# Convolution blocks of 120 tokens with 8 rows of history, and the order of the first slot and of the last products

## The chip, the core and the metric

The kernel runs on one core of a Trainium2 chip. The metric is device time in microseconds (us) of the whole launch, by the median of its runs. A core has TensorE (PE in the rows; PEld is its weight load, which overlaps matmuls), VectorE (DVE), ScalarE (ACT), GpSimd (POOL) and SyncE (SP), which mainly starts transfers. The engines run at the same time, each through its own list of instructions, strictly in the order of that list; they wait for each other and for transfers by semaphores. SPq, ACTq and POOLq are the moments at which a transfer is issued.

## What is computed

A causal convolution over 7 tokens, with softmaxed taps for each of 8 heads, and behind it a routed feed-forward layer with 8 experts of which each token takes the best one:

```python
# x (8, 3584, 192), weight (8 heads, 7 taps)
w = softmax(weight)
out = np.einsum('hk,bskhg->bshg', w, x_unf)      # x_unf: windows of 7 tokens, zeros before the first
x = out.reshape(28672, 192)
logits = x @ w_gate + modality_bias[modality_id]
e_idx = np.argmax(logits, axis=1)
gate_w = softmax(logits)[np.arange(N), e_idx]
for e in range(8):
    h = np.maximum(x[e_idx == e] @ w1[e], 0.0)              # 192 -> 1024
    out[e_idx == e] = gate_w[e_idx == e, None] * (h @ w2[e])  # 1024 -> 192
```

All data is float32. With these inputs nearly all tokens go to experts 6 and 7 (14239 and 13901 of 28672; 532 go to expert 1).

## The kernel before, in words

**Tiles and groups.** A tile is a block of MB = 112 consecutive tokens of one of the 8 sequences, so 3584 / 112 = 32 blocks and 256 tiles. A load takes 4 tiles with 128 rows each: the block and the HALO = 16 rows ahead of it (`load_behind`, L273). The convolution is a matmul with a banded 128 x 112 matrix for each head. Tiles are worked in groups (class `Group`); QUADS_OF_GROUP (L22) gives the loads of each: 19 groups, the last 14 of them of 4 loads, 16 tiles. The first ten groups (WHOLE_X) multiply in plain float32 (`convolve_pair`, L318); the nine behind them split x into a high and a low part `xh`, `xl` and take three products for each head (`convolve`, L309). Then come the gate's logits (`turn`, `gate`, `logits`), the choice of expert (`choose`), a running count by which each token gets a row in a scratch tensor sorted by expert (`place`, two matmuls with `tri` and `ones`), and one indirect transfer for each tile that writes its rows there (`send`, L215, on POOL). The outputs y of the convolution lie in four buffers, each free again when its scatters have landed.

**Slots.** The feed-forward part runs in slots: one expert with 2, 4 or 1 passes of 256 rows, 114 passes in all. A slot loads its weights (`raw`, L674 to L679), splits each into a high and a low part (`w1b`, `w2b`; ACT casts, DVE subtracts, L103 and L104, eight parts, of which 0 to 3 are w1 and 4 to 7 are w2), and fetches its rows by lots of LOT = 2 passes (`bring`, L684: nine transfers, four `near`, four `far`, one `tags`). `turn` transposes a pass on DVE (`tp`) and splits it (`sxh`, `sxl`, `sxs`). A pass has 4 steps; each step has `first` (20 matmuls into `hps`, then `hh` on ACT and `hl` on DVE, of which the next but one step's `hps` needs the end, since there are two such banks) and, two steps later (LAG), `second` (16 matmuls into `po`). After a pass `put` scales its two tiles of 128 rows (`lowp` on ACT, `o` on DVE) and scatters them to the output (L791, on POOL).

**What sets the order.** The groups of chunk 0 (GROUPS_OF_CHUNK, four groups) are worked before the first slot; the others are dealt out over the steps of the slots that run meanwhile (`due`). On all engines a list scheduler sets the final order, except that ACT's is as written while slots run. SP issues weights, lots and x loads in one list: each lot stands behind the weights of the slot before which it was written. The kernel starts with `warm(WARM)`, 50 matmuls on constants, and has 20 more (WARM2) ahead of the first slot. `start(0)` splits parts 0 to 3 of the first slot, then deals out 26 pieces of group work, then turns pass 0; parts 4 to 7 follow behind the first `first`:

```python
for part in range(4 if i == 0 else 8):      # start
    made[i].split(part)
...
cur.first(p, fp)                            # run
if i == step == 0:
    for part in range(4, 8):
        cur.split(part)
...
for sl, *at in lagging:                     # the last two steps' second products
    sl.second(*at)
```

Of the kernel before, what the change touches and what calls it, by code (L numbers as in the profile page):

```python
# [9 lines left out]
F32 = mybir.dt.float32  # L10
F32R = mybir.dt.float32r
BF16 = mybir.dt.bfloat16
I32 = mybir.dt.int32
# [5 lines left out]
P = 128  # L19
MB = 112  # L20
HALO = 16
QUADS_OF_GROUP = (1, 1, 2, 2, 2) + (4,) * 14  # L22
WHOLE_X = 10
# [5 lines left out]
ORDERED = {mybir.EngineType.Activation}  # L29
WARM = 50  # L30
WARM2 = 20
# [4 lines left out]
T = 256  # L36
GROUPS_OF_CHUNK = (4, 3, 2, 2, 2, 2, 2, 2, 0, 0)
SLOTS_OF_CHUNK = (4, 3, 3, 4, 3, 4, 3, 3, 3)
# [8 lines left out]
def conv_then_routed_ffn(ctx, tc, x, weight, modality, w_gate, mod_bias, w1, w2, out):  # L47
    nc = tc.nc
    NB, S, D = x.shape
# [3 lines left out]
    N = NB * S  # L53
    NSB = S // MB
    NG = len(QUADS_OF_GROUP)
# [129 lines left out]
    def make_modality():  # L185
        both = const.tile([MB, 2, E], F32, name="both")
        nc.scalar.dma_start(out=both.rearrange("p m e -> p (m e)"),
                            in_=mod_bias.rearrange("m e -> (m e)").partition_broadcast(MB))
        step = const.tile([MB, E], F32, name="step")
        nc.vector.tensor_tensor(out=step, in0=both[:, 1, :], in1=both[:, 0, :], op=ALU.subtract)  # L190
        rows = N // MB
        ids = raw2[1].rearrange("p c d -> p (c d)")[:, 0:2 * MB * rows // P].bitcast(I32).rearrange("p (q s) -> p q s", s=2 * MB)
        nc.scalar.dma_start(out=ids, in_=modality.bitcast(I32).rearrange("(q p s) -> p q s", p=P, s=2 * MB))
        low = raw2[1].rearrange("p c d -> p (c d)")[:, 2 * MB * rows // P:3 * MB * rows // P].rearrange("p (q s) -> p q s", s=MB)
        nc.vector.tensor_copy(out=low, in_=ids.rearrange("p q (s two) -> p q s two", two=2)[:, :, ::-1, 0])
        mt_ps = ring(ps_t, 4, [MB, rows], F32, "mt_ps", "t")
        for q in range(rows // P):
            nc.tensor.transpose(out=mt_ps[:, q * P:(q + 1) * P], in_=low[:, q, :], identity=ident)
        mt = const.tile([MB, NB, NSB], F32, name="mt")
        with tc.issue_after(state["wg"]):  # L200
            nc.vector.tensor_copy(out=mt.rearrange("p b s -> p (b s)"), in_=mt_ps)
        return both[:, 0, :], step, mt
# [38 lines left out]
    class Group:  # L241


        def __init__(self, g, chunk):
# [13 lines left out]
            assert self.blocks * self.nb == self.tiles and self.b0 + self.nb <= NB  # L258

        def bank(self, use, *args):  # L260
# [12 lines left out]
        def load_behind(self, q, after_band):  # L273
            sb, b0 = self.block + q // 2, self.b0 + q % 2 * 4
            xr = self.x[:, 4 * q:4 * q + 4, :] if self.whole_x else ring(xp, 3, [P, 4, D], F32, "xr")
            if sb == 0:
# [102 lines left out]
        def choose(self):  # L379
# [22 lines left out]
            for i, y in enumerate(self.ys):  # L402
                nc.vector.reciprocal(out=y[0:MB, self.b0:self.b0 + self.nb, 0], in_=den[:, i * self.nb:(i + 1) * self.nb])
                with tc.issue_after(state["scatter"]) if "scatter" in state else nullcontext():
                    nc.gpsimd.iota(y.bitcast(I32)[0:MB, self.b0:self.b0 + self.nb, 1], pattern=[[S, self.nb]],
                                   base=self.b0 * S + (self.block + i) * MB + MB - 1,
                                   channel_multiplier=-1)

        def place(self):
# [4 lines left out]
            ohf = oh.rearrange("p t e -> p (t e)")  # L414
            nc.tensor.matmul(rp[:, 0].rearrange("p t e -> p (t e)"), tri, ohf, start=True, stop=True)
            nc.tensor.matmul(rp[:, 1].rearrange("p t e -> p (t e)"), ones, ohf, start=True, stop=True)
            ad = rt.tile([MB, E * NT], F32, name="ad", tag="ex", bufs=1)[:, 0:E * n].rearrange("p (e t) -> p e t", e=E)
# [20 lines left out]
        def send(self, t0, t1):  # L438
            for t in range(t0, t1):
                scatter(self.chunk, self.idx[:, t:t + 1], self.ys[t // NB][0:MB, self.b0 + t % NB, :])  # L440

# [220 lines left out]
    class Slot:  # L662


        def __init__(self, i, chunk, ent):
            self.i, self.h, self.passes, self.rows, self.ends, self.tags = i, {}, plan[chunk][2] // T, {}, {}, {}
            self.chunk, self.ent, load = chunk, ent, nc.sync
            with tc.issue_after(state["load"]) if "load" in state else nullcontext():
# [55 lines left out]
        def turn(self, k):  # L724
            lot, k0 = divmod(k, LOT)
            tp = ring(sp, 2, [P, NJ + 1, P], F32, "tp")
# [33 lines left out]

        def second(self, k, fp):
            wb = w2b[self.i % 2]
            hh, hl = self.h.pop((k, fp))
            if fp == 0:
                self.po = [ring(ps_g2, 2, [P, 2 * D], F32, "po") for _ in range(NJ)]
            for u in range(2):
                c = 2 * fp + u
                for j, po in enumerate(self.po):
                    js = slice(j * P, (j + 1) * P)
# [11 lines left out]
            if fp == NF // 2 - 1:  # L781
                self.put(self.h.pop(("tag", k)))

        def put(self, tag):
            for j, po in enumerate(self.po):
                gate = tag[:, j, 0:1]
# [10 lines left out]

    plan, tokens, slots, g = [], 0, 0, 0
    for chunk, groups in enumerate(GROUPS_OF_CHUNK):
        tokens += sum(QUADS_OF_GROUP[g:g + groups]) * 4 * MB  # L800
        g += groups
        size = PASSES_OF_SLOT[chunk] * T
        if chunk == len(GROUPS_OF_CHUNK) - 1:
# [69 lines left out]

    lots = [(i, lot) for i, (c, _) in enumerate(order) for lot in range(max(1, plan[c][2] // T // LOT))]

# [13 lines left out]
    def run(i0, i1):  # L889

        lagging, count = [], 0
        for i in range(i0, i1):
# [3 lines left out]
            for step in range(steps):  # L896
                p, fp = divmod(step, NF // 2)
                cur.first(p, fp)
                if i == step == 0:
                    for part in range(4, 8):  # L900
                        cur.split(part)
                lagging.append((cur, p, fp))
# [12 lines left out]
                if step >= (1 if late else 0) and order[far][0] in tables:  # L915
                    make(far)
                lot, end = lots.index((i, p // LOT)), sum(k < i1 for k, _ in lots) - 1
                if min(steps, NF) - step % NF <= 6 or sent(min(lot + 1, end)):
# [69 lines left out]
```

## Time and profile before

| | us |
|---|---|
| median of 3 runs (1249.28 to 1249.97) | 1249.29 |
| the profiled execution, its own time | 1249.29 |
| its span, first to last event | 1247.5 |
| PE busy in it | 1220.0 |
| DVE busy | 988.0 |
| ACT busy | 731.0 |
| POOL busy | 536.4 |

The rows further below come from this one execution. The busy time of PE is modelled: matmuls overlap, so the distance from one start to the next, or the share of the chain of waits, tells what a matmul costs the engine, not its own duration. [...] In the view of stretches the engine columns are busy us and, in brackets, instructions.

### The profile page before, as it was taken

Reading aid. Unit: us, or ns where it says so; the run is one execution under the profiler, and the core shown is the slowest. Engines: PE = TensorE matmul, PEld = TensorE weight load, DVE = VectorE, ACT = ScalarE, POOL = GpSimd, SP = SyncE. Lnnn points to the kernel's source line nnn. Section 1 sums busy time; section 2 is a strip of 40 time slices with the busy share of each in tenths; the row PEclk is TensorE's granted clock in tenths of the full one; section 3 lists DMA queues with packets and bytes.
Section 4 is the critical chain, followed back from the end, with each engine's and each line's share of the span. In section 5 each row is a group of like instructions: output and inputs, shape, how many; then the busy total and the mean of one; then the engine's idle time right before and its main releaser. Section 6 shows DMA issues by size and latency. Waiting matters only on the chain.

```text
span 1247.5 us, 28175 instructions
## 1 busy us (share of the span) xinstructions
PE 1220.0 (98%) x9254; PEld 1202.5 (96%) x9254; DVE 988.0 (79%) x2515; ACT 731.0 (59%) x1602; POOL 536.4 (43%) x564
## 2 busy tenths in 40 slices
PE   9899999999999999999999999999999999999996
PEld 7789999999999999999999999999999999999996
DVE  7688987878888778888888788877886676687894
ACT  2265665656666656665656556656655555556784
POOL 6647753535453453444545343452636221211221
PEclk9899999999999999999999999999999999999998
DMA  7687462543455335535552345423325334795541
GB/s 223 184 199 227 115 148 48 131 110 74 101 151 136 68 92 114 127 77 129 122 129 68 89 95 135 114 65 57 79 57 178 59 74 105 166 207 151 126 99 48
DMA packets 314016, 145.87 MB, mean 117 GB/s; under 512 B 225666, under 2 KB 300027, under 8 KB 313860
## 3 DMA queue, kind: packets, MB, share of 16 engines
q1 hardware_dynamic: 289396, 99.42, 36.7%
q0 software_dynamic: 23232, 44.30, 11.1%
q8 instruction: 74, 1.21, 0.4%
q14 instruction: 82, 0.67, 0.2%
q10 hardware_dynamic: 1232, 0.26, 0.1%
HBM read 118.16 MB, written 51.82 MB: 136 GB/s over the span
## 4 chain that ended last, share of the span: by engine, by line
PE 80%; DVE 8%; DMA 4%; issue 3%; ACT 2%; SPq 1%; POOL 0%; DVEq 0%; ACTq 0%; POOLq 0%
PE hps L752 37%; PE po L772 23%; PE po L776 11%; PE gt L365 4%; PE cv L309 3%; DMA raw<-in_moe_w_dram 2%; PE cv L325 2%; DVE hl L756 1%; DVE w1b L104 1%; DMA xr<-in_x_dram 1%; PE hps L118 1%; DMA routed_rows<-y,idx 1%; SPq L704 1%; DVE xl L104 1%; DVE tp L728 1%
## 5 line engine op out<-in xcount | busy, mean ns | idle before, releaser
L772 PE MATMUL po<-w2b,hh 128*128 128x384 f32 x1824 | 553.4, 354 | 0.9 <-DVE o L790 0.9
L752 PE MATMUL hps<-sxh,w1b 128*128 128x256 f32 x1824 | 481.5, 287 | 4.7 <-DVE hl L756 2.3
L756 DVE SCALAR_TENSOR_TENSOR hl<-hps,hh 128x512 fp32r<-128x512 f32 x456 | 311.2, 685 | 181.8 <-ACT hh L755 178.6
L755 ACT ACTIVATE hh<-hps 128x512 fp32r<-128x512 f32 x456 | 273.0, 599 | 310.3 <-PE hps L752 302.5
L776 PE MATMUL po<-w2b,hl 128*128 128x192 f32 x1824 | 441.7, 252 | 0.0
L215 POOL DMA_INDIRECT routed_rows<-y,idx x256 | 268.3, 1048 | 321.8 <-DVE hl L756 162.0
L791 POOL DMA_INDIRECT out_dram<-o,tags x228 | 239.1, 1049 | 370.2 <-DVE o L790 300.6
L752 PE MATMUL hps<-sxs,w1b 128*128 128x256 f32 x1824 | 363.0, 280 | 0.5 <-DVE sxs L739 0.5
L752 PEld LDWEIGHTS hps<-sxh,w1b 128*128 128x128 f32 x1824 | 343.9, 189 | 11.3 <-DVE hl L756 10.1
L776 PEld LDWEIGHTS po<-w2b,hl 128*128 128x128 f32 x1824 | 345.4, 190 | 0.0
L772 PEld LDWEIGHTS po<-w2b,hh 128*128 128x128 f32 x1824 | 343.9, 189 | 1.4 <-DVE o L790 1.1
L752 PEld LDWEIGHTS hps<-sxs,w1b 128*128 128x128 f32 x1824 | 279.8, 189 | 0.7 <-DVE sxs L739 0.7
L752 PE MATMUL hps<-sxl,w1b 128*128 128x256 f32 x912 | 255.8, 281 | 0.0
L752 PEld LDWEIGHTS hps<-sxl,w1b 128*128 128x128 f32 x912 | 172.8, 189 | 0.2 <-DVE sxl L739 0.2
L104 DVE TENSOR_TENSOR w1b<-raw,w1b 128x512 fp32r<-128x512 f32 x152 | 101.1, 675 | 11.1 <-ACT w1b L103 10.8
L788 ACT ACTIVATE lowp<-po,tags 128x192 f32<-128x192 f32 x228 | 83.6, 418 | 30.3 <-PE po L772 29.7
L103 ACT CAST w1b<-raw 128x512 fp32r<-128x512 f32 x152 | 92.4, 620 | 4.4 <-DMA raw<-in_moe_w_dram 3.7
L104 DVE TENSOR_TENSOR w2b<-raw,w2b 128x384 fp32r<-128x384 f32 x152 | 81.1, 543 | 12.0 <-ACT w2b L103 11.6
L790 DVE SCALAR_TENSOR_TENSOR o<-po,tags,lowp 128x192 f32<-128x192 f32 x228 | 84.3, 410 | 2.3 <-ACT lowp L788 2.3
L737 ACT CAST sxs<-tp 64x128 fp32r<-64x128 f32 x228 | 67.9, 298 | 30.1 <-DVE tp L730 27.3
L103 ACT CAST w2b<-raw 128x384 fp32r<-128x384 f32 x152 | 76.0, 512 | 1.0
L739 DVE TENSOR_TENSOR sxs<-tp,sxs 64x128 fp32r<-64x128 f32 x228 | 65.9, 289 | 9.0 <-ACT sxs L737 0.4
(138 smaller groups left out, 1020.8 us busy)
## 6 DMA issues: line engine op xcount, KB each, us to landing
raw<-in_moe_w_dram SPq DMA_DIRECT2D x38, 768.0 KB
raw<-in_moe_w_dram SPq DMA_DIRECT2D x38, 512.0 KB
raw<-in_moe_w_dram SPq DMA_DIRECT2D x76, 256.0 KB
xr<-in_x_dram SPq DMA_DIRECT2D x36, 384.0 KB
near<-routed_rows SPq DMA_DIRECT2D x212, 64.0 KB
x<-in_x_dram SPq DMA_DIRECT2D x26, 384.0 KB
routed_rows<-filler SPq DMA_DIRECT2D x9, 776.0 KB
far<-routed_rows SPq DMA_DIRECT2D x212, 32.0 KB
```

Of the source, the lines that this page charges most:

```text
L103: nc.scalar.copy(out=hi, in_=raw)
L104: return nc.vector.tensor_tensor(out=lo, in0=raw, in1=f(hi), op=ALU.subtract).ins
L215: state["scatter"] = nc.gpsimd.indirect_dma_start(out=scr, out_offset=bass.IndirectOffsetOnAxis(ap=idx, axis=0), in_=src, in_offset=None,).ins
L737: nc.scalar.copy(out=hi, in_=raw)
L752: nc.tensor.matmul(hps[:, u, :], wa[:, c, fs], mv[z], start=n == 0, stop=n == len(terms) - 1)
L755: nc.scalar.activation(out=hh, in_=hps, func=AF.Relu)
L756: hl_ins = nc.vector.scalar_tensor_tensor(out=hl, in0=hps, scalar=0.0, in1=f(hh), op0=ALU.max, op1=ALU.subtract)
L772: nc.tensor.matmul(po, hh[:, u, js], wb[:, c, :], start=c == 0, stop=c == NF - 1, skip_group_check=True)
L776: nc.tensor.matmul(po[:, 0:D], hl[:, u, js], wb[:, c, 0:D], start=False, stop=False, skip_group_check=True)
L788: nc.scalar.activation(out=lowp, in_=po[:, D:2 * D], func=AF.Copy, scale=gate)
L790: turn_behind(nc.vector.scalar_tensor_tensor(out=o, in0=po[:, 0:D], scalar=gate, in1=lowp, op0=ALU.mult, op1=ALU.add))
L791: st = nc.gpsimd.indirect_dma_start(out=out, out_offset=bass.IndirectOffsetOnAxis(ap=tag.bitcast(I32)[:, j, 1:2], axis=0), in_=o, in_offse ...
```

## The change

A block is now 120 tokens with 8 rows of history (the convolution needs 6). 3584 is no multiple of 120: there are 30 blocks, and the last one's rows end 16 short (CUT; 104 are left, ENDS). Its loads fill the missing rows with zeros by a memset on POOL, its counting matmuls take 104 rows, its scatters send 104. There are 240 tiles and 18 groups: one group of 16 tiles of the second kind (xh, xl) is gone, from the last chunk that has groups. The lookup of modalities is laid out anew (four transfers and a memset for one transfer). WARM is 42 for 50, and such a matmul now has 4 x 120 = 480 columns for 448. Slot 0 fetches its two passes as two lots of one pass each (`self.lot`), and all eight parts of its weights are split ahead of the group work in `start`. The two last steps' second products are worked by tile: all of tile 0, its `put`, then all of tile 1 and its `put`. The plan of slots keeps its size, 114 passes.

```diff
-MB = 112
-HALO = 16
-QUADS_OF_GROUP = (1, 1, 2, 2, 2) + (4,) * 14
+MB = 120
+HALO = 8
+QUADS_OF_GROUP = (1, 1, 2, 2, 2) + (4,) * 13
-WARM = 50
+WARM = 42
-GROUPS_OF_CHUNK = (4, 3, 2, 2, 2, 2, 2, 2, 0, 0)
+GROUPS_OF_CHUNK = (4, 3, 2, 2, 2, 2, 2, 1, 0, 0)
...
-    NSB = S // MB
+    NSB = -(-S // MB)
+    CUT = NSB * MB - S
+    ENDS = MB - CUT
...
+            if sb == NSB - 1:
+                nc.gpsimd.memset(xr[0:Q], 0.0)
+                ld = nc.sync.dma_start(out=xr[CUT:P], in_=x[b0:b0 + 4, sb * MB - HALO:S, :].rearrange("b s d -> s b d"))
...
+            for h, wt in enumerate((tri, ones)):
+                for lo, hi, rows in self.runs():
+                    nc.tensor.matmul(rp[:, h].rearrange("p t e -> p (t e)")[:, lo * E:hi * E], wt[0:rows], ohf[0:rows, lo * E:hi * E],
+                                     start=True, stop=True)
...
+            self.chunk, self.ent, self.lot, load = chunk, ent, 1 if i == 0 else LOT, nc.sync
...
-            k0, k1 = lot * LOT, min(lot * LOT + LOT, self.passes)
+            k0, k1 = lot * self.lot, min((lot + 1) * self.lot, self.passes)
...
-                if i == step == 0:
-                    for part in range(4, 8):
-                        cur.split(part)
...
-        for sl, *at in lagging:
-            sl.second(*at)
+        for j in range(NJ):
+            for sl, *at in lagging:
+                sl.second(*at, tiles=[j])
...
-        for part in range(4 if i == 0 else 8):
+        for part in range(8):
             made[i].split(part)
```

Three places show what this moves. Names: `w1b_89`, `w2b_91` and `raw_0` are the first slot's weights, `raw_1` the second's; line numbers are each kernel's own.

ACT, around the splits of the first slot, before:

```order
L328 COPY y_218<-cv 112x2x8x24 x3
L103 CAST w1b_89<-raw_0_85 128x512 x4
L328 COPY y_218<-cv 112x2x8x24
L737 CAST sxh<-tp 128x256
L737 CAST sxs<-tp 64x128 x2
L755 ACTIVATE hh<-hps 128x512
L103 CAST w2b_91<-raw_0_87 128x2x192 x4
L755 ACTIVATE hh<-hps 128x512
```

and in the change:

```order
L342 COPY y_202<-cv 120x2x8x24 x3
L105 CAST w1b_89<-raw_0_85 128x512 x4
L105 CAST w2b_91<-raw_0_87 128x2x192 x4
L342 COPY y_202<-cv 120x2x8x24
L759 CAST sxh<-tp 128x256
L759 CAST sxs<-tp 64x128 x2
L777 ACTIVATE hh<-hps 128x512 x2
L759 CAST sxh<-tp 128x256
```

The four casts of w2 moved from behind the first `hh` to a place ahead of a copy out of the convolution.

DVE, from the first slot's first `hl` on, before:

```order
L756 SCALAR_TENSOR_TENSOR hl<-hps,hh 128x512
L104 TENSOR_TENSOR w2b_91<-raw_0_87,w2b_91 128x2x192 x4
L756 SCALAR_TENSOR_TENSOR hl<-hps,hh 128x512
L728 STREAM_TRANSPOSE tp<-near 128x256
L730 STREAM_TRANSPOSE tp<-far 128x128
L739 TENSOR_TENSOR sxl<-tp,sxh 128x256
L739 TENSOR_TENSOR sxs<-tp,sxs 64x128 x2
L756 SCALAR_TENSOR_TENSOR hl<-hps,hh 128x512 x3
```

and in the change:

```order
L778 SCALAR_TENSOR_TENSOR hl<-hps,hh 128x512 x2
L750 STREAM_TRANSPOSE tp<-near 128x256
L761 TENSOR_TENSOR sxl<-tp,sxh 128x256
L752 STREAM_TRANSPOSE tp<-far 128x128
L761 TENSOR_TENSOR sxs<-tp,sxs 64x128 x2
L778 SCALAR_TENSOR_TENSOR hl<-hps,hh 128x512 x2
```

The subtractions for w2 are no longer between the first two `hl`; the turn of pass 1 (`tp` from `near` and `far`) still stands between the second `hl` and the third, but its rows are now those of a second lot.

SP, from the end of the first slot's first lot on, before (the lot of both passes ends with `tags`; what follows is slot 1):

```order
L704 DMA tags<-routed_rows 128x4x2
L669 TENSOR_LOAD tab
...
L674 DMA raw_1_86<-in_moe_w_dram 128x1024
...
L679 DMA raw_1_88<-in_moe_w_dram 128x8x192
L689 TENSOR_LOAD tab
...
L704 DMA near<-routed_rows 32x16x32
```

and in the change:

```order
L726 DMA tags<-routed_rows 128x2x2
L691 TENSOR_LOAD tab
...
L696 DMA raw_1_86<-in_moe_w_dram 128x1024
...
L701 DMA raw_1_88<-in_moe_w_dram 128x8x192
L711 TENSOR_LOAD tab
...
L726 DMA near<-routed_rows 32x8x32
```

The first `near` behind slot 1's weights now belongs to slot 0's pass 1 (32x8x32, half a lot), and slot 1's own lot (32x16x32) comes behind that.

## Rows read from the trace of the kernel before

**Rows 1.** The page: busy time of each engine, its share of the span, instructions.

```profile
PE 1220.0 (98%) x9254; PEld 1202.5 (96%) x9254; DVE 988.0 (79%) x2515; ACT 731.0 (59%) x1602; POOL 536.4 (43%) x564
```

**Rows 2.** Stretches of the span (from:to, length, then busy us of each engine with its instructions, granted clock, DMA share, GB/s).

```profile
48.00:53.30 5.30, 0.32 (x4) 0.12 (x2) 2.24 (x4) 2.65 (x5) 4.08 (x5) 0.91 1.03 312
...
140.00:1184.00 1044.00, 1041.20 (x7987) 1035.27 (x7986) 834.37 (x2040) 632.06 (x1382) 435.87 (x444) 1.00 0.46 108
```

**Rows 3.** The chain of waits in order of time, three pieces from the stretches 255 to 272 and 395 to 470: start, us on the chain, what (one counting matmul; the three products of one head; the twelve of one gate of 8 tiles).

```profile
271.35 0.06 PE rp L415
...
398.23 0.54 PE cv L309 x3
...
436.81 1.40 PE gt L365 x12
```

**Rows 4.** Groups of instructions by line and shape: the first of the three products of a head, nine groups by 8, and the gate's matmuls of the twelve later groups by 24.

```profile
L365 PE MATMUL gt<-gx,wg_parts 128*128 128x256 f32 x288 | 38.7, 282 | 1.8 <-DVE gx L104 1.5 <-ACT gx L103 0.3
...
L309 PE MATMUL cv<-xh,band_hi 128*112 128x384 f32 x72 | 25.4, 352 | 0.2 <-ACT xh L103 0.2
```

**Rows 5.** The end in order of time, on ACT, DVE and POOL: start, us, engine, line, operation, in brackets the idle time before it and its releaser.

```profile
1237.40 0.73 ACT L788 ACTIVATE lowp<-po,tags 128x192 f32<-128x192 f32 x2 [2.53 <-PE po L772]
1237.85 0.74 DVE L790 SCALAR_TENSOR_TENSOR o<-po,tags,lowp 128x192 f32<-128x192 f32 x2 [2.26 <-ACT lowp L788]
1238.55 0.98 POOL L791 DMA_INDIRECT out_dram<-o,tags  x1 [4.65 <-DVE o L790]
1239.83 0.99 POOL L791 DMA_INDIRECT out_dram<-o,tags  x1 [0.30 <-issue]
```

**Rows 6.** The start in order of time: the 50 warm-up matmuls, one weight load of them among the early ones, the 40 later ones, the loads of x behind the band matrices, the first convolutions.

```profile
1.16 11.88 PE L118 MATMUL hps<-ones 112*112 112x448 bf16 x50 [1.16 <-DVE ones L113]
...
3.82 0.22 PEld L118 LDWEIGHTS <-ones 112*112 112x112 bf16 x1 [0.16 <-issue]
...
4.19 0.22 PEld L118 LDWEIGHTS <-ones 112*112 112x112 bf16 x1 [0.16 <-issue]
...
4.57 8.06 PEld L118 LDWEIGHTS <-ones 112*112 112x112 bf16 x40 [0.16 <-issue]
...
11.12 3.25 SPq L280 DMA_DIRECT2D x<-in_x_dram  x6
...
13.10 3.29 PE L325 MATMUL cv<-x,band 128*112 128x96 f32 x32
```

**Rows 7.** POOL's scatters into the scratch rows in order of time: the first one, then the last two of chunk 0.

```profile
22.89 1.12 POOL L215 DMA_INDIRECT routed_rows<-y,idx  x1 [5.48 <-DVE ad L418]
...
51.92 0.94 POOL L215 DMA_INDIRECT routed_rows<-y,idx  x1 [0.30 <-issue]
53.17 1.29 POOL L215 DMA_INDIRECT routed_rows<-y,idx  x1 [0.30 <-issue]
```

**Rows 8.** SP's issues in order of time: slot 0's lot (near to tags), slot 1's weights, slot 1's lot.

```profile
56.18 2.04 SPq L704 DMA_DIRECT2D near<-routed_rows  x4
...
61.50 0.40 SPq L704 DMA_DIRECT2D tags<-routed_rows  x1
63.41 0.37 SPq L674 DMA_DIRECT2D raw<-in_moe_w_dram  x1
...
66.92 4.50 SPq L704 DMA_DIRECT2D near<-routed_rows  x4
...
74.16 0.39 SPq L704 DMA_DIRECT2D tags<-routed_rows  x1
```

**Rows 9.** ACT in order of time around the first slot.

```profile
51.70 1.14 ACT L103 CAST w1b<-raw 128x512 fp32r<-128x512 f32 x2 [2.34 <-DMA raw<-in_moe_w_dram]
52.74 0.47 ACT L328 COPY y<-cv 112x384 f32<-112x384 f32 x1
...
66.58 1.75 ACT L103 CAST w2b<-raw 128x384 fp32r<-128x384 f32 x4
```

**Rows 10.** DVE in order of time: pass 0's last transpose and subtractions, the first `hl`, pass 1's last transpose.

```profile
63.50 0.30 DVE L730 STREAM_TRANSPOSE tp<-far 128x128 f32<-128x128 f32 x1
64.17 0.61 DVE L739 TENSOR_TENSOR sxs<-tp,sxs 64x128 fp32r<-64x128 f32 x2 [0.36 <-ACT sxs L737]
66.59 0.69 DVE L756 SCALAR_TENSOR_TENSOR hl<-hps,hh 128x512 fp32r<-128x512 f32 x1 [1.81 <-ACT hh L755]
...
70.03 0.27 DVE L730 STREAM_TRANSPOSE tp<-far 128x128 f32<-128x128 f32 x1
```

**Rows 11.** PE in order of time: ten float32 convolution matmuls ahead of the first slot, the first matmul of step 2, the first of step 4 (pass 1).

```profile
60.54 1.79 PE L325 MATMUL cv<-x,band 128*112 128x192 f32 x10
...
67.34 0.39 PE L752 MATMUL hps<-sxh,w1b 128*128 128x256 f32 x1 [0.59 <-DVE hl L756]
...
72.47 0.39 PE L752 MATMUL hps<-sxh,w1b 128*128 128x256 f32 x1
```

**Rows 12.** Packets that the DMA engines moved from 64 to 71 us, then from 71 to 76.5 us (the rows of a lot are packets of 128 and 8 bytes, weights are packets of 4096 and 768 bytes).

```profile
DMA packets 1145, 1.69 MB, mean 242 GB/s; under 512 B 48, under 2 KB 889, under 8 KB 1145
...
DMA packets 4167, 0.97 MB, mean 177 GB/s; under 512 B 3824, under 2 KB 4087, under 8 KB 4167
```

**Rows 13.** PE alone, by stretches of 1 us: length, busy (instructions), granted clock, DMA share, GB/s.

```profile
58.00:59.00 1.00, 1.00 (x7) 0.50 1.03 208
59.00:60.00 1.00, 1.00 (x10) 0.90 0.76 112
```

More of the change, by code (lines that the diff above doesn't have):

```diff
@@ L258, in __init__, with rows @@
             assert self.blocks * self.nb == self.tiles and self.b0 + self.nb <= NB
+        def rows(self, i):
+            return ENDS if self.block + i == NSB - 1 else MB
         def bank(self, use, *args):
@@ L405, in choose, with runs @@
                     nc.gpsimd.iota(y.bitcast(I32)[0:MB, self.b0:self.b0 + self.nb, 1], pattern=[[S, self.nb]],
-                                   base=self.b0 * S + (self.block + i) * MB + MB - 1,
+                                   base=self.b0 * S + (self.block + i) * MB + self.rows(i) - 1,
                                    channel_multiplier=-1)
+        def runs(self):
+            if self.rows(self.blocks - 1) == MB:
+                return [(0, self.tiles, MB)]
+            return [(i * self.nb, (i + 1) * self.nb, self.rows(i)) for i in range(self.blocks)]
         def place(self):
@@ L439, in send @@
             for t in range(t0, t1):
-                scatter(self.chunk, self.idx[:, t:t + 1], self.ys[t // NB][0:MB, self.b0 + t % NB, :])
+                rows = self.rows(t // NB)
+                scatter(self.chunk, self.idx[0:rows, t:t + 1], self.ys[t // NB][0:rows, self.b0 + t % NB, :])
     chunk_of = [c for c, n in enumerate(GROUPS_OF_CHUNK) for _ in range(n)]
@@ L724, in turn @@
         def turn(self, k):
-            lot, k0 = divmod(k, LOT)
+            lot, k0 = divmod(k, self.lot)
             tp = ring(sp, 2, [P, NJ + 1, P], F32, "tp")
@@ L759, in first, with second @@
             self.h[k, fp] = hh, hl
-        def second(self, k, fp):
+        def second(self, k, fp, tiles=range(NJ)):
             wb = w2b[self.i % 2]
-            hh, hl = self.h.pop((k, fp))
-            if fp == 0:
+            hh, hl = self.h[k, fp]
+            if fp == 0 and tiles[0] == 0:
                 self.po = [ring(ps_g2, 2, [P, 2 * D], F32, "po") for _ in range(NJ)]
@@ L767, in second @@
                 c = 2 * fp + u
-                for j, po in enumerate(self.po):
+                for j, po in [(j, self.po[j]) for j in tiles]:
                     js = slice(j * P, (j + 1) * P)
@@ L781, in second, with put @@
             if fp == NF // 2 - 1:
-                self.put(self.h.pop(("tag", k)))
-        def put(self, tag):
-            for j, po in enumerate(self.po):
+                self.put(self.h["tag", k], tiles)
+        def put(self, tag, tiles):
+            for j, po in [(j, self.po[j]) for j in tiles]:
                 gate = tag[:, j, 0:1]
@@ L795, in put @@
                 tc.add_to_no_dep_group("out", st)
[L798 removed]
+    plan, tokens, slots, g, seen = [], 0, 0, 0, 0
     for chunk, groups in enumerate(GROUPS_OF_CHUNK):
[L800 removed]
         g += groups
+        brought = sum(QUADS_OF_GROUP[:g]) * 4 * MB - (CUT * NB if g == NG else 0)
+        tokens, seen = tokens + brought - seen, brought
         size = PASSES_OF_SLOT[chunk] * T
@@ L872, in make @@
             made.append(Slot(len(made), chunk, tables[chunk][:, k, :]))
-    lots = [(i, lot) for i, (c, _) in enumerate(order) for lot in range(max(1, plan[c][2] // T // LOT))]
+    lots = [(i, lot) for i, (c, _) in enumerate(order) for lot in range(max(1, plan[c][2] // T // (LOT if i else 1)))]
     def bring(n):
@@ L916, in run @@
                     make(far)
-                lot, end = lots.index((i, p // LOT)), sum(k < i1 for k, _ in lots) - 1
+                lot, end = lots.index((i, p // cur.lot)), sum(k < i1 for k, _ in lots) - 1
                 if min(steps, NF) - step % NF <= 6 or sent(min(lot + 1, end)):
```

27 lines of the change are left out of this document (15 added, 12 removed).

## The prediction

> **What bounds the kernel now.** I read the page's busy times first [rows 1]: PE is busy for 1220.0 of 1247.5 us, and the reader should see that no other engine comes near. Shares over the whole span hide stages, so the stretches come next [rows 2]: from 140 to 1184 PE is busy for 1041.2 of 1044.0 us while DVE has 834, so in the middle every matmul counts in full. What is left lies at the ends, and the sharpest piece is from 48.0 to 53.3, where PE does 0.32 us of work. The chain of waits [rows 3] gives the path's price of each piece of convolution work, and the groups by line and shape [rows 4] say how many there are. Then I read the two ends in order of time: the end on ACT, DVE and POOL [rows 5], the start on PE [rows 6], POOL's scatters [rows 7], SP's issues [rows 8], ACT, DVE and PE around the first slot [rows 9 to 11], and what the DMA engines move there [rows 12]. The clock row by row is last [rows 13].
>
> All terms are made against the profiled execution. Its own time, 1249.29, is also the median of the runs, and its span is 1247.5; I take the 1.8 us around the span as unchanged.
>
> **A group less.** The nine xh/xl groups make 72 high products, 8 each, and the twelve later groups 288 gate matmuls, 24 each [rows 4]. On the chain three products of a head cost 0.54 us, the twelve gate matmuls of 8 tiles 1.40, and a counting matmul 0.06 [rows 3]. One group is 8 × 0.54 + 2 × 1.40 + 2 × 0.06 = 7.24. It was worked while PE was full [rows 2], so it is on the path. The last group now takes four counting matmuls for two, +0.12. Columns per matmul don't change with the block (24 per tile), so the other groups cost what they did: **−7.1**. The passes stay 114. DVE, ACT and POOL lose the group's work too, under PE's cover. New there is a POOL memset ahead of each of two loads of the last groups, and SP, in order, waits with the weights and lots behind them. Loads run well ahead of their use, so I take 0; if that cover is gone I allow up to 2 us, from two scatter-sized POOL operations of about 1 us [rows 7].
>
> **The last products by tile.** Now both `o` are ready at about the same time, the second at 1237.85 + 0.74 = 1238.59, and POOL sends both behind that, at 1238.55 and 1239.83 [rows 5]. By tile, the first has gone by then, and the second can start as soon after its own `o` as POOL takes up a released scatter, about 0.3 us, at 1238.87. The matmuls are the same in number. 1239.83 − 1238.87: **−1.0**. Between 0 (the second `o` a microsecond later) and −1.3 (the distance of the two scatters).
>
> **The warm-up.** The early matmuls come 0.37 us apart (3.82 to 4.19), then 40 in 8.06 us, 0.20 each, and the convolutions start at 13.10 [rows 6]. With 480 columns for 448 these are 0.40 and 0.216; 42 of them end at about 11.8, 1.3 sooner. The x loads stand behind the band matrices and are issued at 11.12, and the first convolution follows warm-up without a wait, so I count the whole 1.3, though only for what hangs on it: POOL's chain of scatters. That chain runs from 22.89 to 54.46 with 24 scatters at a steady distance (1.25 us in the last two), and one of 112 rows takes 0.94 [rows 7] where one of 128 rows takes 0.98 to 0.99 [rows 5]. For 120 rows I add 0.02 each: +0.5. Slot 0's first `near`, issued at 56.18 [rows 8], comes at 56.18 − 1.3 + 0.5 = 55.4. The modality lookup is the last thing on PE ahead of the first convolution; with four transfers for one it may come later than the warm-up's end, and then this 1.3 is gone. Nothing waited there before, and I take 0.
>
> [...] No row of the kernel before shows a 120-row transfer.
>
> **The first slot's order.** Two things meet here.
>
> First, pass 0 comes sooner. Its lot is half as large. The full second lot, moved from about 71 to 76.5 as 4167 small packets [rows 12], tells that half of one saves up to 2.6 us; I take 2.0, since each transfer's own start is not halved. Pass 0's last transpose stood at 63.50 [rows 10]; 63.5 − 0.8 (the sooner issue) − 2.0 = 60.7. The four w2 casts (1.75 us [rows 9]) are now ahead of the copy of y that PE waits for at 53.3, and lengthen that idle time, but what ends last is still the rows of pass 0. Step 2's first matmul moves from 67.34 [rows 11] to about 64.8. The w2 splits no longer stand between the first two `hl`, which were at 66.59 and 69.07 at the far side of those subtractions.
>
> Second, pass 1 comes later. Its rows used to be in the one lot. Now they are behind slot 1's weights on SP. Those were issued at 63.41 [rows 8], and until 71 the DMA engines move hardly anything else: 1145 packets, 48 of them under 512 bytes [rows 12]. SP reaches them about 1.5 us sooner (0.8 and the shorter lot, whose issue gives less than its landing); they are through at 69.5, and half a lot behind them takes 2.6: 72.1. DVE and ACT stand in order at pass 1's transposes, so nothing of steps 2 and 3 behind them goes on either. From pass 1's last transpose at 70.03 [rows 10] to step 4's first matmul at 72.47 [rows 11] it took 2.44. So step 4 starts at 72.1 + 2.44 = 74.5, 2.0 later. By 64.8 + (72.47 − 67.34) = 69.9 PE is through with what stands ahead of it, and it waits some 4.5 us. At 74.5 PE has done less than at 72.47 before: of the ten float32 products ahead of the first slot, 1.79 us together [rows 11], six are not yet done (1.0), against two `po` products (0.35) done in advance, +0.6. Together **+2.6**; its ends are −1.9 (no wait, below) and +5.
>
> **Sum:** 1249.29 − 7.1 − 1.0 + 2.6 = **1243.8**.
>
> **Rivals.**
> *B, the wait also lowers the clock.* After the idle stretch up to 53.3 [rows 2] PE ran at 0.50 until about 59.15: the second from 58 to 59 has 0.50, the next 0.90 [rows 13]. So 5.9 us of matmuls ran at half speed, about 3.0 lost. A second idle stretch of 4.5 us behind step 3 is nearly as long as that one of 5.0. If it lowers the clock too: 1243.8 + 3.0 = 1246.8. Against it: the idle may come out shorter, or be broken by a few late products. [...]
>
> *C, pass 1 arrives in time.* Packets of the second lot may be let in between the weights' packets, or the weights be through sooner. For it: slot 1's lot was issued from 66.92 on [rows 8], well before the weights were through. Against it: of its packets hardly any came before 71 [rows 12]. Then step 4 starts at 69.9, 2.5 sooner than 72.47; with the 0.6: 1249.29 − 8.1 − 2.5 + 0.6 = 1239.3.
>
> *D, slower: the second lot lands much later.* Slot 1's weights go out as one block ahead of it, and x loads and scatters share the engines. If the rows of pass 1 land 5.0 us later than I say (77.1), and the clock drops as well, it is 1246.8 + 5.0 = 1251.8; without the drop it takes 8.0 us (80.1). Slot 1's whole lot, behind the same weights, was in by 76.5 [rows 12], so this is unlikely.
>
> *E, the change doesn't do what it says:* the group's 7.1 us come back as waits, because DVE (834 of 1044) or the loads set the pace where the group stood: 1249.29 − 1.0 + 2.6 = 1250.9.
>
> **How the numbers follow.** About 0.2%, 2.5 us, is what a measurement of this kernel can tell from no change: faster is under 1246.8, slower over 1251.8. A has 0.42, B 0.26 (it lies on the bound: half faster, half same), C 0.20, D 0.06, E 0.04, and 0.02 is for others, half faster and half same. Faster 0.42 + 0.13 + 0.20 + 0.01 = 0.76; same 0.13 + 0.04 + 0.01 = 0.18; slower 0.06. The range goes from just below C, 1238.8, to 0.8 above B, 1247.6, and leaves out D, E and what memset and landing times add to B.
>
> **What would show it.** Right: 64 high products where 72 stood, 264 gate matmuls; the first convolution at about 11.8; slot 0's first `near` at about 55.4; DVE idle ahead of pass 1's `tp`, released by its rows, and step 4's first matmul near 74.5; the last scatter 0.3 us behind its `o`. A granted clock of 0.50 between 74 and 80 is B. Step 4 by 71 is C. Wrong: PE idle over 3 us between 140 and 1184, or a step 4 beyond 77.

## The result, and the profile after

The changed kernel took 1258.54 us (median of 4 runs, 1258.1 to 1259.77), the kernel before 1249.63 on the same chip: a ratio of 1.0073, 95% interval 1.0061 to 1.0085. It is 8.9 us slower, where 5.5 us faster was forecast. The profiled execution took 1259.77, its span is 1258.1.

The page, PE's share, as [rows 1]:

```profile
PE 1218.9 (97%) x9198; PEld 1201.9 (96%) x9198; DVE 972.8 (77%) x2476; ACT 722.2 (57%) x1581; POOL 529.2 (42%) x546
```

The span grew by 10.6 us, and PE is idle for 11.7 more. Its busy time fell by only 1.1, although a group is gone, because more of it fell into stretches with a granted clock (PEclk, TensorE's, as a share of full speed) of 0.50: 19.0 us up to PE's last matmul, where the kernel before has 5.9, so some 6.5 us more were lost to the clock. The loss is at both ends. First the start on PE, as [rows 6], and then the instruction on DVE that PE waits for (start, us, engine, line, operation, in brackets idle time and its releaser):

```profile
1.17 11.55 PE L120 MATMUL hps<-ones 120*120 120x480 bf16 x42 [1.17 <-DVE ones L115]
18.77 0.62 PE L206 MATMUL mt_ps<-ident,raw 120*120 120x120 f32 x2 [6.05 <-DVE raw L203]
19.19 5.61 PE L339 MATMUL cv<-x,band 128*120 128x96 f32 x32
```

```profile
18.34 0.29 DVE L203 CAST raw<-raw 120x240 f32<-120x240 int32 x1 [9.97 <-DMA raw<-in_moe_modality_id_dram]
```

The convolutions start at 19.19, not 11.8: the modality ids are late. In the kernel before, their cast comes at 7.46, and the band matrices are issued at 7.56:

```profile
7.46 0.72 DVE L195 CAST raw<-raw 128x224 f32<-128x224 int32 x1 [0.35 <-DMA raw<-in_moe_modality_id_dram]
7.56 0.40 SPq L161 DMA_DIRECT2D band<-tap_lines  x1
```

The band matrices are now late as well. They are issued at 10.65, and the x loads behind their landing at 18.41 (11.12 before, [rows 6]), from SP in order of time:

```profile
10.65 0.40 SPq L163 DMA_DIRECT2D band<-tap_lines  x1
18.41 3.48 SPq L294 DMA_DIRECT2D x<-in_x_dram  x6
```

From 8 to 10 us the DMA engines move this and no more (packets, bytes, rate; then ACT's queue alone):

```profile
DMA packets 46, 0.05 MB, mean 26 GB/s; under 512 B 0, under 2 KB 45, under 8 KB 46
...
q10 hardware_dynamic: 45, 0.04, 6.2%
```

That is 45 packets of 960 bytes in 2 us, one every 44 ns: 6.2% of sixteen engines, about what one engine's share would be, a sixteenth or 6.25%. The view doesn't name the engine; that it is one is worked out from this share. From 14 to 18 us the last 65 packets of the band matrices (q1; 958 had gone from 11.8 to 14) and 64 packets of the ids (q10) take 6.9% together, again about one engine's share:

```profile
DMA packets 129, 0.09 MB, mean 23 GB/s; under 512 B 67, under 2 KB 129, under 8 KB 129
q10 hardware_dynamic: 64, 0.06, 4.3%
q1 hardware_dynamic: 65, 0.03, 2.6%
```

Behind these waits the granted clock of PE is lower. Stretches of PE (length, busy, granted clock, DMA share, GB/s):

```profile
16.00:18.00 2.00, 0.00 (x0) 0.70 0.07 22
...
20.00:22.00 2.00, 2.00 (x12) 0.50 0.96 318
...
58.00:59.00 1.00, 1.00 (x6) 0.50 0.92 228
...
65.00:66.00 1.00, 0.54 (x2) 0.50 0.35 93
...
84.00:85.00 1.00, 0.00 (x0) 1.00 0.15 2
86.00:87.00 1.00, 0.34 (x1) 0.50 0.76 106
90.00:91.00 1.00, 1.00 (x7) 0.50 0.34 90
92.00:93.00 1.00, 1.00 (x11) 1.00 0.90 279
```

It falls four times (once ahead of the tail before, [rows 2, 13]): at the first convolutions, twice ahead of the first slot, and behind 80 us. POOL's chain, as [rows 7], and SP's issues, as [rows 8], carry the first delay on:

```profile
31.07 1.19 POOL L223 DMA_INDIRECT routed_rows<-y,idx  x1 [6.44 <-DVE ad L439]
...
62.23 1.00 POOL L223 DMA_INDIRECT routed_rows<-y,idx  x1 [0.30 <-issue]
```

```profile
65.19 1.91 SPq L726 DMA_DIRECT2D near<-routed_rows  x4
...
71.73 0.37 SPq L696 DMA_DIRECT2D raw<-in_moe_w_dram  x1
...
75.24 2.90 SPq L726 DMA_DIRECT2D near<-routed_rows  x4
```

The first scatter is 8.2 later than before, slot 0's first `near` 9.0. Then pass 1, on DVE and on PE:

```profile
74.38 1.49 DVE L778 SCALAR_TENSOR_TENSOR hl<-hps,hh 128x512 fp32r<-128x512 f32 x2 [0.93 <-ACT hh L777]
83.78 0.45 DVE L750 STREAM_TRANSPOSE tp<-near 128x256 f32<-128x256 f32 x1 [7.92 <-DMA near<-routed_rows]
```

```profile
86.66 1.01 PE L794 MATMUL po<-w2b,hh 128*128 128x384 f32 x2 [6.51 <-ACT hh L777]
...
88.28 0.67 PE L774 MATMUL hps<-sxh,w1b 128*128 128x256 f32 x1
```

DVE stands 7.92 us at pass 1's rows, which are behind slot 1's weights on SP, PE is idle for 6.51, and step 4 starts at 88.28 (72.47 before, [rows 11]). The end, on POOL, as [rows 5]:

```profile
1246.88 0.98 POOL L813 DMA_INDIRECT out_dram<-o,tags  x1 [3.81 <-DVE o L812]
1248.17 0.98 POOL L813 DMA_INDIRECT out_dram<-o,tags  x1 [0.30 <-issue]
```

From the last scatter's end to the end of the span it is now 1258.1 - 1249.15 = 8.95 us, before 1247.5 - 1240.82 = 6.68.

**A ledger.** `hl` has 456 instructions in every kernel, in the same order, so the lateness of the n-th one against the kernel before shows where time goes (from the two traces, us): the 1st +7.8, the 2nd +6.1, the 3rd (behind the pause) +14.9, the 5th +17.0, the 17th +14.7, the 237th +14.1, the 333rd +9.2, the last +9.2; the span +10.6. So the head costs about 15, some 2 of it taken back by the 17th, where PE in the kernel before waited 2.8 itself; the group less, between the 237th and the 333rd, gives back 4.9; the end costs 1.4.

### The profile page after: what moved, and what is told of

Same layout as the page of the kernel before. It is cut to its first block, busy times and chain, and to the rows that moved or that the text cites. A ratio compares the mean times of both kernels' runs of the same rounds, so it can differ in the third digit from the quotient of the medians.

```text
span 1258.1 us, 28006 instructions
## 1 busy us (share of the span) xinstructions
PE 1218.9 (97%) x9198; PEld 1201.9 (96%) x9198; DVE 972.8 (77%) x2476; ACT 722.2 (57%) x1581; POOL 529.2 (42%) x546
## 3 DMA queue, kind: packets, MB, share of 16 engines
q0 software_dynamic: 22464, 44.31, 11.3%
## 4 chain that ended last, share of the span: by engine, by line
PE 81%; DVE 6%; DMA 5%; issue 3%; ACT 2%; SPq 1%; POOL 1%; ACTq 0%; DVEq 0%; POOLq 0%
PE hps L774 37%; PE po L794 24%; PE po L798 11%; PE gt L379 4%; PE cv L323 3%; PE cv L339 2%; DMA routed_rows<-y,idx 1%; DMA xr<-in_x_dram 1%; DVE hl L778 1%; DMA raw<-in_moe_w_dram 1%; DVE w1b L106 1%; DMA raw<-in_moe_modality_id_dram 1%; DVE xl L106 1%; SPq L726 1%; DVE tp L750 1%
## 5 line engine op out<-in xcount | busy, mean ns | idle before, releaser
L223 POOL DMA_INDIRECT routed_rows<-y,idx x240 | 263.8, 1099 | 315.8 <-DVE hl L778 179.7
L106 DVE TENSOR_TENSOR w1b<-raw,w1b 128x512 fp32r<-128x512 f32 x152 | 101.1, 675 | 12.5 <-ACT w1b L105 12.5
L759 ACT CAST sxh<-tp 128x256 fp32r<-128x256 f32 x114 | 46.8, 410 | 46.6 <-DVE tp L750 46.4
```

The source lines that it names most:

```text
L106: return nc.vector.tensor_tensor(out=lo, in0=raw, in1=f(hi), op=ALU.subtract).ins
L223: state["scatter"] = nc.gpsimd.indirect_dma_start(out=scr, out_offset=bass.IndirectOffsetOnAxis(ap=idx, axis=0), in_=src, in_offset=None,).ins
L759: nc.scalar.copy(out=hi, in_=raw)
```

## Experiments

Theory 1 is that the ids are late because one DMA engine takes all their rows, theory 2 that the pause ahead of pass 1 is the second half lot behind slot 1's weights; their rivals stand with the runs. On three of the chips that the runs fell on (4, 10 and 15) the kernel before took 1287 to 1290: there PE also waits, between 20 and 300 us, for 11 to 23 us in all for what the profile calls issue or remote, and neither the kernel before nor the changed kernel has such a wait in the traces above. The expectations below read this as instructions that come late or programs that are loaded slowly; no run shows what is waited for. PE's waits in h1 (us in total, times, longest):

```profile
PE hps L120 <- remote: 7.0, 1, 7.0
PE gt L380 <- issue: 6.3, 10, 1.1
PE cv L340 <- issue: 5.1, 3, 1.9
```

Ratios from those chips are not set against ratios from the first one; positions in the traces up to 20 us, and distances between neighbouring instructions, are. The kernel before took 1249.51 on chip 13 (g1 to g6).

**The ids spread (a1, c1, d1, h1: one kernel).** The 29 whole blocks as 28 and 1:

```diff
-            nc.scalar.dma_start(out=ids[0:whole, q], in_=bass.AP(words.tensor, words.offset + at, [[2 * MB, NSB - 1], [2 * S, NB // 2], [1, 2 * MB]]))
+            for s0, s1 in ((0, NSB - 2), (NSB - 2, NSB - 1)):
+                nc.scalar.dma_start(out=ids[s0 * NB // 2:s1 * NB // 2, q], in_=bass.AP(words.tensor, words.offset + at + 2 * MB * s0, [[2 * MB, s1 - s0], [2 * S, NB // 2], [1, 2 * MB]]))
```

> The changed kernel, with the 29 whole blocks of modality ids fetched as 28 and 1 (six transfers on ACT's queue for four). Theory 1: the 116-row transfer runs its rows one after another on one DMA engine, some 44 ns each, 240 rows about 10.4 us, and holds back the last rows of the band matrices too; in this form the rows are spread, the ids are in by about 12 us, the first convolution starts at 12 to 13 instead of 19.19, the clock doesn't fall ahead of it, and the time is 8 us shorter, about 1250.5. The pause of 6.5 us ahead of pass 1 stays. Rival 1: the lookup is late because of the number of transfers issued on ACT's queue and because the later ones stand behind the cast of wgs; with six issues the first convolution is at 19 or later and the time 1258 to 1260.

> The changed kernel as it is, again, so that the next three have it on the same chip. 1.007 of the kernel before if the chip loads its programs as fast as the first one did; on the chip of the runs a1, a2, a3 and b1 everything was 25 to 40 us longer, and there the ratio isn't known.

> The changed kernel with the ids as 28 and 1 blocks, as in a1. Theory 1: about 8 us shorter than the changed kernel on the same chip (first convolution 6 us sooner, and about 2 us of matmuls at half clock behind it saved), 1.000 to 1.001 of the kernel before; the pause ahead of pass 1 stays. Rival 1: no shorter.

The first convolution moved to 13.19, 13.05, 12.62 and 12.89 in the four traces, although two more transfers are issued; the changed kernel again (c0) had 19.03. Theory 1 holds, rival 1 falls. From the first convolution to the first scatter it takes 10.1 to 10.6 us in them, 11.88 in the changed kernel and 9.79 before; in a1 the cast of the ids and the convolution stand at

```profile
11.98 0.28 DVE L204 CAST raw<-raw 120x240 f32<-120x240 int32 x1 [3.75 <-DMA raw<-in_moe_modality_id_dram]
13.19 3.81 PE L340 MATMUL cv<-x,band 128*120 128x96 f32 x32
```

In time, on chip 15: c0 0.9983 of the kernel before (0.9955 to 1.0011), so there the changed kernel is not slower, and the 0.7% stands for the first chip alone; c1 0.9902 (0.9872 to 0.9932), some 10 us below c0; a1, on chip 4, 0.9913 (0.9881 to 0.9944). The other two, on chips 10 and 15:

> [...] Theory 1 on a chip like the one of the prediction: 1250 to 1251, 1.000 to 1.001 of the kernel before (the changed kernel has 1.007 there). Where instructions come late again: 0.990, as in c1.

> The changed kernel with only the ids spread over more engines, on a chip where the kernel before takes 1249 to 1250 as at the prediction. Theory 1: the first scatter of POOL 8.2 us sooner than in the changed kernel, the pause ahead of pass 1 as there: 8 us below 1258.5, about 1250.5, 1.000 to 1.002 of the kernel before. Rival 5: what is gained ahead of the first slot is lost as the pause ahead of pass 1 gets longer by it, 1254 to 1258.

0.9896 (0.9859 to 0.9932) and 0.9888 (0.9855 to 0.992). What the spread ids alone are worth on a chip like the first stays open. The pause from the second to the third `hl` stayed (below).

**One engine, two, four (b1, g1, g2).** The kernel before with its one transfer of 128 rows split, here 127 + 1, then 122 + 6 and 124 + 4:

```diff
-        nc.scalar.dma_start(out=ids, in_=modality.bitcast(I32).rearrange("(q p s) -> p q s", p=P, s=2 * MB))
+        words = modality.bitcast(I32).rearrange("(q p s) -> p q s", p=P, s=2 * MB)
+        for lo, hi in ((0, 127), (127, P)):
+            nc.scalar.dma_start(out=ids[lo:hi], in_=words[lo:hi])
```

That 127 rows go to one engine, 122 to two and 124 to four was the author's assumption ahead of these runs; the traces show packets and the queue's share, not which engine.

> The kernel before, with its one transfer of modality ids (128 rows) split into 127 rows and 1 row; nothing else changed. Theory 1: 127 rows of twice 224 words go through one engine one after another, about 254 times 42 ns = 10.7 us, the first convolution moves from 13.1 to 16 or 17 and the clock may fall ahead of it: 1253 to 1256. Rival 1: one more transfer changes nothing, 1249 to 1250.

> The kernel before, its transfer of modality ids split into 122 rows and 6 rows. [...] Then 244 packets of some 42 ns are shared by two engines, about 5.1 us instead of 10.3 with one; the cast of the ids (7.46 in the kernel before, 128 rows) comes at about 11, and the convolutions start at about 13 to 14. Rival 1b, any second transfer is slow to start, whatever its rows: the cast as late as with 127 rows, about 19.

> As g1 with 124 rows and 4 rows. Theory 1: 4 engines (31 has no divisor), 248 packets of some 42 ns, about 2.6 us; the cast of the ids at 8.5 to 9, the first convolution at 13.1 as in the kernel before. Rival 1b: the cast about 19.

All packets from 8 to 10 us, for 127 + 1, 122 + 6 and 124 + 4:

```profile
DMA packets 53, 0.05 MB, mean 24 GB/s; under 512 B 0, under 2 KB 53, under 8 KB 53
```

```profile
DMA packets 106, 0.09 MB, mean 47 GB/s; under 512 B 0, under 2 KB 106, under 8 KB 106
```

```profile
DMA packets 155, 0.14 MB, mean 69 GB/s; under 512 B 9, under 2 KB 154, under 8 KB 155
```

53, twice 53, and with 124 rows about three times, since most of them are in by 9.5; from 8 to 9 us alone it is 26, 53 and 106, one, two and four times 26. Over the 2 us the ids' queue has 6.8%, 13.6% and 18.8% of sixteen engines (6.25% would be one). By 6.8%, 53 packets in 2 us take 41 ns of an engine each, so the 26, 53 and 106 are an estimated 1.1, 2.2 and 4.3 us of engine time in 1 us. The cast of the ids comes at 19.34, 13.00 and 10.50, the first convolution at 20.20, 14.63 and 13.84 (13.10 before). A second transfer as such does little, since 124 + 4 has one too and its first convolution is 0.74 later than before; the rate differs with the rows of the first, 127, 122 (2 × 61) or 124 (4 × 31). Why it does is not shown. b1 took 1.0049 of the kernel before (1.0014 to 1.0085), some 6 us, as forecast, though its first convolution came 3 us later than the 16 to 17 expected; g1 took 1251.9 and g2 1248.59 in one run each, beside 1249.51. The casts of g1 and g2 come 2 us later than expected: most of their packets come from 7 us on, when the kernel before has nearly all of its 256 in (its queue moved 272 packets, some of them not ids, from 6 to 7).

**Slot 0's rows (a2, a3, c2, d2: one lot; c3, d3: second lot ahead of slot 1's weights; d4: only the halves, in the kernel before).**

```diff
-            self.chunk, self.ent, self.lot, load = chunk, ent, 1 if i == 0 else LOT, nc.sync
+            self.chunk, self.ent, self.lot, load = chunk, ent, LOT, nc.sync
```

```diff
-        bring(lots.index((i, 0)))
+        bring(lots.index((i, 0)) + (i == 0))
```

> The changed kernel, with slot 0's two passes fetched as one lot again; the ids as changed. Theory 2: the pause behind step 3 (6.5 us of no work and 5.1 us at half clock behind it) is the second half lot behind slot 1's weights. With one lot step 4 starts about 5.1 us behind step 2 instead of 13.1, pass 0 starts about 2.5 later; no second fall of the clock: 1258.5 - 8.0 + 2.5 - 2.0, about 1251. The first convolution stays at 19.2. Rival 2: the DMA engines are loaded in that stretch by x loads, scatters and weights whatever the lot, and a whole lot lands as late as the two halves: 1257 to 1259.

> The changed kernel with both edits: ids as 28 and 1 blocks, and one lot for slot 0. If theories 1 and 2 hold and the costs add, about 1243; the removed group and the tail then show in full. If one pause only takes the place of the other, 1248 to 1251.

> As c1, and slot 0's rows as one lot, as in a3. Theory 2: the pause of some 6.5 us and the 5 us at half clock behind it go, pass 0 starts 2.5 us later: 6 to 8 us shorter than c1, 0.994 to 0.996 of the kernel before. Rival 2 (what is gained is lost as pass 0 waits longer for its whole lot, and the clock falls there instead): within 2 us of c1.

> As c1 (two lots of one pass for slot 0), but the second one is issued on SP ahead of slot 1's weights. Theory 2: the pause goes as in c2, and pass 0 keeps its early start: 1 to 2 us shorter than c2, 0.993 to 0.995 of the kernel before. Rival 2: the pause is due to something else than the weights ahead of the lot: as c1, 1.000.

> As d1, slot 0's rows as one lot. On the slow chips this gave back what it took (0.991 for 0.990), because pass 0 started later by as much. Theory 2 where the pause ahead of pass 1 is some 6 us: 0.994 to 0.996, 6 us below d1. Rival 2, the exchange of one wait for the other everywhere: within 2 us of d1.

> As d1, slot 0's second lot issued ahead of slot 1's weights. Theory 2: no pause ahead of pass 1 and pass 0 as early as in d1: 1 to 2 us below d2, 0.993 to 0.995. Rival 3: slot 1's weights, now later by the nine issues of a lot (some 5 us), become what the start of slot 1 waits for, and the time is that of d2 or more.

> The kernel before, with only slot 0's rows as two lots of one pass, the second behind slot 1's weights. Theory 2: step 2 starts up to 2.5 us sooner, step 4 comes 8 to 13 us behind step 2 for 5.1, and with the clock the kernel is 2 to 6 us slower, 1.002 to 1.005. Rival 2: pass 0's earlier start pays for it, 0.998 to 1.000.

The distance from the second `hl` to the third, in us, is the pause, since 2.65 is what the kernel before has:

| | second to third `hl` | ratio to the kernel before |
|---|---|---|
| changed kernel, first chip; c0 | 11.47; 4.70 | 1.0073; 0.9983 |
| halves, ids spread: a1, c1, d1, h1 | 8.07, 7.22, 9.95, 7.73 | 0.9913, 0.9902, 0.9896, 0.9888 |
| halves alone in the kernel before: d4 | 5.99 | 0.9976 (0.9949 to 1.0004) |
| one lot: a2; with ids: a3, c2, d2 | 2.66; 2.66, 2.66, 2.66 | 0.9968; 0.9916, 0.9912, 0.9936 |
| second lot ahead, ids: c3, d3, g3 | 3.72, 3.48, 3.95 | 0.9920, 0.9899, 1.0011 |

So theory 2 is right on the cause: the pause is there wherever the second half lot stands behind the weights; with one lot it is gone, and with the second lot ahead 0.8 to 1.3 of it remain. On its price it was wrong: undoing it gave no time on those chips (c2 to c1 0.9912 to 0.9902, within both intervals; a3 to a1 likewise; d2 is behind d1), and the halves alone (d4) cost nothing that shows, where 1.002 to 1.005 was expected. On a chip like the first the price was not measured by itself. Pass 0 is earlier with half a lot: the first `hl` stood at 76.16 in c1 and 78.39 in c2. Rival 2, one wait for the other, is what these chips show. With the second lot ahead, the weights are late instead (rival 3): in g3 PE waits for an `o`, and ACT, shortly before, for slot 1's w1 to land; that the one delays the other is argued from the order of ACT and DVE:

```profile
81.61 0.45 PE L795 MATMUL po<-w2b,hh 128*128 128x384 f32 x1 [1.97 <-DVE o L813]
```

```profile
77.14 0.62 ACT L105 CAST w1b<-raw 128x512 fp32r<-128x512 f32 x1 [1.72 <-DMA raw<-in_moe_w_dram]
```

From its third `hl` to the 17th g3 takes 51.0 us, the kernel before 48.6. Set against the kernel before as in the ledger, g3 has its first `hl` at +0.1, the 3rd at -0.3, the 17th at +2.1, the 237th at +3.0, the 333rd at -1.2 and the last at -0.5, and its span is 1.2 longer: the head's delay is gone, the group less gives 4.2, and small losses behind the 3rd `hl` and at the end take it back.

**All of the slot's order undone (h2):** one lot, and parts 4 to 7 behind the first products, as the kernel before has both.

> The changed kernel with the ids spread, slot 0's rows as one lot, and parts 4 to 7 of its weights split behind the first products again: what remains of the change is the block of 120, the group less, the shorter warm-up and the last products by tile. Theory 2: the first slot runs as in the kernel before (step 4 some 5 us behind step 2), the group less is worth 5.5 us as in the trace of the changed kernel, the rest about 0: 1243 to 1245, 0.995 to 0.997 of the kernel before. Rival 2: the slot's new order isn't what costs, and this comes out as h1.

0.9916 (0.9882 to 0.9949) beside h1's 0.9888 (0.9855 to 0.992), on chip 15 again: as rival 2 says there, and open on a chip like the first.

**The last products (g3: old order, on top of d3; g6: order by tile alone, in the kernel before).** The edit of g3, and g6 the reverse with the two functions' `tiles`:

```diff
-        for j in range(NJ):
-            for sl, *at in lagging:
-                sl.second(*at, tiles=[j])
+        for sl, *at in lagging:
+            sl.second(*at)
```

> As d3 (ids spread, slot 0's second lot ahead of slot 1's weights), and the last products in their old order. In the eleven traces of kernels with the order by tile the launch ends 10.1 to 11.3 us behind PE's last matmul, in the three with the old order 9.7 to 9.85. Theory 4: the order by tile itself makes the end longer: here 9.6 to 9.9, and the last scatter to the end 6.5 to 6.7 instead of 7.8 to 9.0. Rival 4: it gains the 1 us forecast and the block of 120 or something else makes the end longer: here 11 to 12.

> The kernel before with only the last products by tile. Theory 4: the end lies 10.1 to 11.3 behind PE's last matmul (9.85 in the kernel before), the last scatter 7.8 to 9.0 ahead of the end. Rival 4: 8.9, the 1 us forecast is gained. In time either is under the spread of the runs on these chips.

POOL's last two scatters in g6 (span 1247.7):

```profile
1238.41 0.99 POOL L791 DMA_INDIRECT out_dram<-o,tags  x1 [3.80 <-DVE o L790]
1239.70 1.00 POOL L791 DMA_INDIRECT out_dram<-o,tags  x1 [0.30 <-issue]
```

and in g3 (span 1248.7):

```profile
1238.09 0.98 POOL L814 DMA_INDIRECT out_dram<-o,tags  x1 [4.66 <-DVE o L813]
1239.38 0.98 POOL L814 DMA_INDIRECT out_dram<-o,tags  x1 [0.30 <-issue]
```

Theory 4 falls. The order by tile brings the last scatter from 2.19 to 1.34 us behind PE's last matmul (g6), and g6's launch ends 7.0 behind the end of that scatter, near the 6.5 to 6.8 of the other kernels with 112 rows, and 9.3 behind PE's last matmul (9.8 before). g3 has the old order, and its launch ends 8.3 behind the scatter, 11.5 behind PE's last matmul, like the kernels with blocks of 120 and the order by tile (7.8 to 9.0 and 10.1 to 11.3) but for the 0.85 by which its scatter is later. What the end hangs on is something of the 120-row program that no run here isolates. In time: g6 0.9993 (0.9983 to 1.0002), no change; g3 1.0011 (1.0002 to 1.0021). The kernel before took 1249.51 there and 1249.63 beside the changed kernel, so spread ids, the second lot ahead and the old last products together (g3) take back 0.6% of the 0.7%; the part of each is not measured there. None of the kernels was shown to beat the kernel before on such a chip. On chips 4, 10 and 15 all ten runs with spread ids beat it, by 0.6 to 1.1%; why they do there is open.

## Why the prediction was wrong

**The modality lookup was the step that failed.** The prediction saw that it is the last thing on PE ahead of the first convolution, and wrote "Nothing waited there before, and I take 0", with 1.3 as the price if it were late. The cast of the ids came 10.9 us later than before (18.34 for 7.46), the first convolution 6.1 later than before and 7.4 later than forecast, and the matmuls behind it ran at a granted clock of 0.50 until 23 us: 8.2 at the first scatter. The 1.3 bounded only the gain, not the wait. The prediction saw the number of transfers, four for one, and didn't ask how their rows are shared out. What sets that share is not shown; the runs show the rates. The 116 rows, from a source of 29 blocks, moved 45 packets in 2 us; with the blocks as 28 and 1 the first convolution came 5.8 to 6.6 sooner (12.62 to 13.19 for 19.19); and b1, g1 and g2 moved 26, 53 and 106 packets in 1 us. With scatters of 120 rows the wait for the last of them was no longer: from the last scatter's start to `near` 62.23 to 65.19, 2.96, and 3.01 before [rows 7, 8].

**Pass 1 behind slot 1's weights** was the right mechanism and the sum was too small: PE was idle for 6.5 us, not 4.5, and step 4 came 13.1 us behind step 2's start (75.21), where 9.7 was forecast (64.8 to 74.5). Rival B came with it: the clock was 0.50 from 85 to 91.8, 5.1 us of matmuls, about 2.6 lost, for 3.0 forecast. From the second `hl` to the third it takes 11.5 us in one trace of this kernel and 4.7 in the other (c0); what sets that length is open, and A's fixed 2.0 was not a term that could be had from one trace.

**The group less** was sized at 7.1 and gave 4.9 between the 237th and the 333rd `hl`, and 5.5 from the 17th to the last; g3 gave 4.2 and 2.6. The prediction wrote "the other groups cost what they did", but 192 products of this kind now stand 196.3 ns apart on the average, 189.8 before (all of PE from the 17th `hl` on), 1.2 us, and 264 gate matmuls 120.8 for 119.6, 0.3: with these, 7.1 would be 5.6. g3 and g6, with 120 and 112 rows, have 195.6 and 187.3. The rise is nearly all in the first product of three, 235.0 for 217.8; the others stand 179.3 and 174.6 for 177.8 and 173.9. The weight load ahead of that first product takes longer; of the kernel before and after (busy us, mean ns):

```profile
L309 PEld LDWEIGHTS cv<-xh,band_hi 128*112 128x112 f32 x72 | 12.6, 175 | 0.5 <-ACT xh L103 0.5
```

```profile
L323 PEld LDWEIGHTS cv<-xh,band_hi 128*120 128x120 f32 x64 | 11.7, 182 | 0.2 <-ACT xh L105 0.2
```

That the load sets the distance is not shown: it grew by 7 ns and the distance by 17.

**The last products by tile** gave 0.85 of the 1.0 forecast up to the last scatter (1.34 us behind PE's last matmul in g6 and in the changed kernel, for 2.19), held at POOL's distance of 1.29, not by the second `o`. Behind it the launch ended 2.3 later than before, which no step of the prediction had.

**The warm-up** was to end at 11.8; it ended at 1.17 + 11.55 = 12.72. The prediction took from one trace that the matmuls come 0.37 us apart until 4.57 and 0.20 apart from then on [rows 6]. Here the wide spacing, 0.40, lasts until 6.42, and only 28 of the 42 come at the narrow one, 0.21:

```profile
6.42 5.86 PEld L120 LDWEIGHTS <-ones 120*120 120x120 bf16 x28 [0.18 <-issue]
```

In the same kernel again (c0) the narrow spacing starts at 4.39, and the warm-up ends at 11.67; over all traces it starts at 4.4 to 7.6. So the 1.3 us can't be read from one execution; with the ids spread the first convolution came at 12.5 to 13.2, for 13.1 before.

**Right:** POOL's chain grew by 0.8 (8.2 to 9.0) for 0.5; and pass 0 came sooner with half a lot (from `near` to the first `hl` 9.19, 10.41 before [rows 8, 10]; to step 2's start 10.0 for 11.2, where 9.4 was forecast; what a transfer's own start takes no run shows).

Adding up: 6.1 and 2.1 for the ids, 0.8 for the scatters, -1.1 up to step 2's first matmul (65.19 to 75.21, before 56.18 to 67.34), 7.9 up to step 4, -6.6 from there to PE's last matmul, 1.4 behind it: 10.6, the growth of the span.

## What to carry to other kernels

When a change alters the shape of a transfer, look in the trace at what rate its packets go, for the small ones in the head above all: here 127 rows, and 116 rows from a source of 29 blocks, went at 53 and 45 packets in 2 us, where the queue of the 128 rows moved 272 in 1 us. When a lot is halved to start sooner, look at what its second half is now queued behind, and don't price that queue by one trace: here two traces of one kernel gave 11.5 and 4.7 us. And a term forecast as "nothing waits there" needs the price of the wait, not only of the gain that is lost.

## What was not expected of the hardware

A transfer with 127 or 116 rows moved a packet every 38 or 44 ns (53 and 45 in 2 us), about one engine's share (6.8% and 6.2% of sixteen). With the 116 rows another queue's transfer, the band matrices, was late too: from 14 to 18 us their last 65 packets went along with 64 of the ids, and from their issue at 10.65 to the x loads behind them it took until 18.41, 7.8 us, for 3.6 before. The same kernel took 1249 us on some chips and 1287 to 1290 on others, where PE's waits for issue and remote add up to 11 to 23 us of the first 300; what it waits for there is open. And the launch ends 7.8 to 9.0 us behind the end of the last scatter in every trace of a 120-row kernel and 6.5 to 7.0 in every one of a 112-row kernel, whatever the order of the last products.
